# Gathering the next expert's rows earlier in an mLSTM-plus-routing kernel

## Chip, core and metric

One core of a Trainium2 chip. The metric is the device time in microseconds of one execution; for the kernel before it is 405.84 us, the median of three (404.99 to 406.05). One more execution was recorded by the hardware profiler; its span is 402.9 us, and all positions in time below are counted from the start of that span.

The core's engines run side by side, each with its own queue of instructions: TensorE (PE in the profile; its weight loads are PEld), VectorE (DVE), ScalarE (ACT), GpSimd (POOL), and SyncE (SP), which issues transfers. [...]

## What is computed

First an mLSTM cell over `(4, 8, 768, 40)`, whose output, as 3072 rows of 320 numbers, is then routed to one of eight experts by a hash of the token:

```python
def _moe_ref(x, token_ids, w1, w2) -> np.ndarray:
    N, D = x.shape                       # 3072, 320
    E = w1.shape[0]                      # 8; w1 is (8, 320, 1024), w2 is (8, 1024, 320)
    expert_idx = token_ids * np.int64(2654435761) % np.int64(E)
    out = np.zeros((N, D), dtype=np.float32)
    for e in range(E):
        mask = expert_idx == e
        if not mask.any():
            continue
        xe = x[mask]
        h = np.maximum(xe @ w1[e], 0.0)
        out[mask] = h @ w2[e]
    return out.astype(np.float32)
```

All of it is in float32. The change lies where the mLSTM ends and the experts begin.

## The kernel before

The mLSTM writes its rows to `x_rows` (`x_d`) in device memory. Each expert gathers the rows that belong to it (three tiles of 128 and 32 remainders, 416 in all), turns them so that the 320 features lie on the partitions, and runs two layers.

Expert 0 is special. Its rows are gathered before the last 256 rows have been stored; what it has of those comes as a product with a table of ones (`om`), and is added at the end. `spin0` runs products that nobody reads.

```python
        rows_by_table(0, 0)
        xo = back(LB, NB - 1)
        rows_by_table(0, 1)
        rows_by_table(0, 2)
        finish(LB, NB - 1, xo)()                  # stores the last rows to x_d
        for i, j in enumerate((NJ, *range(NJ))):
            ...
            for db in range(2):
                nc.tensor.transpose(tp[:, db, :n], xg0[:n, j, db * P : (db + 1) * P], ident[:n, :n])
            nc.scalar.copy(xg0[:n, j, Dm:], xg0[:n, j, 2 * P : Dm])
            nc.tensor.transpose(tp[:, 2, :n], xg0[:n, j, 2 * P :], ident[:n, :n])
            nc.scalar.copy(xT0[:, :, j * P : j * P + n], tp[:, :, :n])       # L904
            if i < DB:
                rows_by_table(1, i)
            if i == DB - 1:
                spin0(1)
        spin0(2)
        for db in range(DB):
            nc.vector.tensor_tensor(xT0[:, db, :], xT0[:, db, :], om[db][:, :CAP], op=ALU.add)   # L911
```

The turn of a tile for the later experts. For expert 1 a small copy on VectorE first doubles the last 64 columns (`copied` is false); from expert 2 on ScalarE has done that before.

```python
    def turn(xg, dst, on_act, copied=False):
        tp = mps.tile([P, DB, P], F32, name="tp", tag="bank")
        for db in range(2):
            nc.tensor.transpose(tp[:, db, :], xg[:, db * P : (db + 1) * P], ident[:])
        if not copied:
            nc.vector.tensor_copy(xg[:, Dm:], xg[:, 2 * P : Dm])             # L944
        nc.tensor.transpose(tp[:, 2, :], xg[:, 2 * P :], ident[:])
        ...                                                                  # copy to dst, ScalarE or VectorE
```

Layer 1 of expert 0 goes over four pairs of feature blocks. `between(fp)` is where a turn may be put in: inside the even pairs, and after the odd ones.

```python
            if fp % 2 == 0:
                for i in range(2):
                    whole(i, True)                # L968, four products
                between(fp)
                halves(False)                     # L961
                for i in range(2):
                    out(i)
            else:
                halves(True)
                for i in range(2):
                    whole(i, False)
                    out(i)
                between(fp)
```

Layer 2 calls `between(0)` after its first plain product, `between(1)` after the middle of a scheme of seven products with sums, and `between(2)` at its end:

```python
        scatter(zp, idx(2), True)
        between(0)
        ...
        product(yb, s2, t2, False)
        nc.vector.tensor_tensor(u2[:], yb, p1[:], op=ALU.add)                # L1148
        between(1)
        product(xb, s1, t1, False)
        nc.vector.tensor_tensor(u3[:], xa, u2[:], op=ALU.add)                # L1151
        nc.vector.tensor_tensor(z1[:, DH:], xb, u3[:], op=ALU.add)           # L1152
        product(ya, a[0][1], half(1, 0), False)
        nc.scalar.copy(z0[:, :DH], ya)
        product(xa, a[1][1], t4, False)
```

And the loop over the experts with what comes before it. `fetch(e)` gathers on GpSimd (L919); `sums_of_w2` is four GpSimd operations (L1105); `turns(1)` is a list of four turns: tiles 0, 1, 2 and the remainders; `sums_of_x` is five VectorE operations on the turned rows of the next expert.

```python
        sums = sums_of_w2(W[0][2])
        fetch(1)

        for piece in weight_slices(1):
            piece(nc.scalar)
        ...
        for e in range(E):
            ...
            ahead = turns(e + 1) if e + 1 < E else []

            def one(fp):
                if ahead and (e > 0 or fp != 0 or len(ahead) < 4):
                    ahead.pop(0)()

            def after(j):
                if j == (e == 0) and e + 1 < E:
                    xss[e + 1] = sums_of_x(xTs[e + 1])
                one(j)
                ...
            if e == 0:
                layer1(W[e], xTs[e], h, CAP, one)
            else:
                layer1_pairs(W[e], wsums, xTs[e], xss[e], h, one)
            ...
            layer2_pair(W[e], sums, h, cols_of(s_idx, e * NJ), after)
```

A scheduler may place an engine's instructions in another order than the program's, so the built kernel's order is read beside the code.

Of the kernel before, what the change touches and what calls it, by code (L numbers as in the profile page):

```python
# [22 lines left out]
def kernel(  # L23
# [30 lines left out]
    E, _, F = moe_w1.shape  # L54
# [9 lines left out]
    DB = len(dch)  # L64
# [52 lines left out]
    def weight_slices(e):  # L117

        W[e], slices = weights(moe_w1[e], moe_w2[e], wpools[e % 3 > 0], w2pools[e % 6 > 0])
        return slices  # L120
# [8 lines left out]
    with tc.tile_pool(name="gates", bufs=1) as gp, \  # L129
# [107 lines left out]
        def piece(z, j, r, src, eng):  # L237
            if eng is nc.scalar:
                nc.scalar.copy(z[r, j, :], src)
            else:  # L240
                nc.gpsimd.tensor_copy(z[r, j, :], src)
# [449 lines left out]
        one = gp.tile([P, 2, 1], F32, name="one")  # L691
# [188 lines left out]
        def rows_by_table(k, db):  # L880
            nc.tensor.matmul(
                om[db][:, :CAP], lhsT=xl[:, k, db * P : (db + 1) * P], rhs=ones0[:, k, :], start=(k == 0), stop=(k == 1),
                skip_group_check=True,
            )


        def spin0(n):
            idle = ps.tile([P, CAP], F32, name="idle", tag="tr", bufs=4)
            for _ in range(n):
                nc.tensor.matmul(idle[:], lhsT=ident[:], rhs=W[0][0][:, 0, :CAP], start=True, stop=True)  # L890
# [6 lines left out]
        for i, j in enumerate((NJ, *range(NJ))):  # L897
            n = RM if j == NJ else P
            tp = ps.tile([P, DB, P], F32, name="tp0", tag="tr", bufs=4)
# [4 lines that stand above are left out]
            nc.scalar.copy(xT0[:, :, j * P : j * P + n], tp[:, :, :n])  # L904
            if i < DB:
                rows_by_table(1, i)
            if i == DB - 1:
                spin0(1)
        spin0(2)
        for db in range(DB):  # L910
            nc.vector.tensor_tensor(xT0[:, db, :], xT0[:, db, :], om[db][:, :CAP], op=ALU.add)  # L911

# [5 lines left out]
    def gather(xg, idx):  # L918
        nc.gpsimd.indirect_dma_start(  # L919
            out=xg, out_offset=None, in_=x_d[:, :], in_offset=bass.IndirectOffsetOnAxis(ap=idx, axis=0),  # L920
        )

    def scatter(zp, idx, apart):
        zo = xp.tile([P, Dm], F32, name="zo", bufs=4)
        nc.scalar.copy(zo[:], zp[:])
        send(zo, idx, apart)
# [11 lines left out]
# [8 lines that stand above are left out]
        if on_act:  # L946
            nc.scalar.copy(dst, tp[:])
        else:
            nc.vector.tensor_copy(dst, tp[:])
        return tp  # L950
# [56 lines left out]
    def sums_of_w1(w1t):  # L1007

        a = [[w1t[:, k, :].rearrange("p (a i f) -> p i a f", i=2, f=P)[:, i] for k in range(2)] for i in range(2)]
        s1, s2, s3, s4 = s = [xp.tile([P, FB // 2, P], F32, name=f"ws{i}", bufs=1) for i in range(1, 5)]  # L1010
        ops = ((s1, a[1][0], a[1][1], ALU.add), (s2, s1[:], a[0][0], ALU.subtract),
               (s3, a[0][0], a[1][0], ALU.subtract), (s4, a[0][1], s2[:], ALU.subtract))
        return s, [lambda o=o: nc.gpsimd.tensor_tensor(o[0][:], o[1], o[2], op=o[3]) for o in ops]  # L1013
# [86 lines left out]
    def sums_of_w2(w2t):  # L1100

        b = [[w2t[:, k::2, c * DH : (c + 1) * DH] for c in range(2)] for k in range(2)]
        t1, t2, t3, t4 = (xp.tile([P, FB // 2, DH], F32, name=f"t{i}", bufs=1) for i in range(1, 5))
        for d, x, y in ((t1, b[0][1], b[0][0]), (t2, b[1][1], t1), (t3, b[1][1], b[0][1]), (t4, b[1][0], t2)):
            nc.gpsimd.tensor_tensor(d[:], x, y[:] if y in (t1, t2) else y, op=ALU.subtract)  # L1105
        return t1, t2, t3, t4
# [56 lines left out]
    def cols_of(t, c0):  # L1163
        return lambda j: t[:, c0 + j : c0 + j + 1]

    with tc.manual_schedule():
        xgs, xTs, remT, hrem = {}, {0: xT0}, {}, {}

        def fetch(e):
            if e % EG == 0 or e == 1:  # L1170
                xgs[-1 - e // EG] = xp.tile([P, DB * P], F32, name="xr")
            xgs[e] = xp.tile([P, NJ, DB * P], F32, name="xg", bufs=3)
            for j in range(NJ):
                gather(xgs[e][:, j, :Dm], cols_of(g_idx, e * NJ)(j))
            if e % EG == 0 or e == 1:
                gather(xgs[-1 - e // EG][:, :Dm], cols_of(g_idx, NR + e // EG)(0))

        def turns(e):
            xT = xTs[e] = xp.tile([P, DB, CAP], F32, name="xT")

            def tile_of(j):
                turn(xgs[e][:, j, :], xT[:, :, j * P : (j + 1) * P], j % 2 == 1, e > 1)

            def remainder():
                i = e % EG
                if i == 0 or e == 1:
                    remT[e // EG] = xp.tile([P, DB, P], F32, name="remT")
                    turn(xgs[-1 - e // EG], remT[e // EG][:], True, e > 1)
                nc.scalar.copy(xT[:, :, NM:], remT[e // EG][:, :, i * RM : (i + 1) * RM])

            return [lambda j=j: tile_of(j) for j in range(NJ)] + [remainder]

        def rest(g):
            zp = mps.tile([P, Dm], F32, name="zp", tag="bank")
            for fb in range(FB):
                for i in range(EG):
                    nc.tensor.matmul(
                        zp[i * RM : (i + 1) * RM, :], lhsT=hrem[g][:, i, fb, :], rhs=W[g * EG + i][2][:, fb, :],
                        start=(fb == 0), stop=(fb == FB - 1),
                    )  # L1200
            scatter(zp, cols_of(s_idx, NR + g)(0), True)

        sums = sums_of_w2(W[0][2])
        fetch(1)


        for piece in weight_slices(1):
            piece(nc.scalar)
        wsums, pieces, xss = None, [], {}
        for e in range(E):  # L1210
            g, i = e // EG, e % EG
            if e + 2 < E:
                fetch(e + 2)
            if e > 0:
                sums = sums_of_w2(W[e][2])
            h = xp.tile([P, FB, CAP], F32, name="h", bufs=1)
            if i == 0:
                hrem[g] = xp.tile([P, EG, FB, RM], F32, name="hrem")
            ahead = turns(e + 1) if e + 1 < E else []

            def one(fp):
                if ahead and (e > 0 or fp != 0 or len(ahead) < 4):
                    ahead.pop(0)()

            def after(j):
                if j == (e == 0) and e + 1 < E:
                    xss[e + 1] = sums_of_x(xTs[e + 1])
                one(j)
                if j == 0 and i == EG - 1:
                    rest(g)  # L1230

            if e + 1 < E:
                wnext, pieces = sums_of_w1(W[e + 1][0])
# [4 lines that stand above are left out]
            for piece in pieces:  # L1238
                piece()
            pieces = []  # L1240
            nc.scalar.copy(hrem[g][:, i], h[:, :, NM:])
            layer2_pair(W[e], sums, h, cols_of(s_idx, e * NJ), after)
            wsums = wnext

            if e + 2 < E:
                for j in range(NJ):
                    nc.scalar.copy(xgs[e + 2][:, j, Dm:], xgs[e + 2][:, j, 2 * P : Dm])
                if (e + 2) % EG == 0:
                    xr = xgs[-1 - (e + 2) // EG]
                    nc.scalar.copy(xr[:, Dm:], xr[:, 2 * P : Dm])  # L1250
            if e + 3 < E:
                slices = weight_slices(e + 3)
                if e == 0:
                    slices[1:1] = weight_slices(2)
                for piece in slices:
                    piece()
# [51 lines left out]
```

## Time and profile before

| engine | busy, us | share of the 402.9 us |
|---|---|---|
| TensorE, products | 378.4 | 94% |
| TensorE, weight loads | 311.6 | 77% |
| VectorE | 221.3 | 55% |
| GpSimd | 201.3 | 50% |
| ScalarE | 148.8 | 37% |

The mean clock granted to TensorE was 0.983 of full speed. TensorE's products in layer 1 of expert 0 begin at 167.82 us; the last scatter of output rows starts at 395.92 us.

A line of the timeline gives start, duration (both in us), engine, line, operation, target and sources, shape, and how many instructions are merged; in brackets stand the idle time of the engine just before, and what ended it. A line of waits gives who waited for whom: total us, times, the longest. A line of the table by windows gives a stretch and its length, then the busy time and number of instructions of PE, PEld, DVE, ACT and POOL, the granted clock, the share of the DMA engines and GB/s.

### The profile page before, as it was taken

To read this page: it belongs to the slowest core of one execution; us is meant where nothing else is said; L and a number is where in the kernel's file an instruction comes from. 1 tells how busy PE (TensorE), PEld (TensorE's weight loads), DVE (VectorE), ACT (ScalarE), POOL (GpSimd) and SP (SyncE) were. 2 spreads that over 40 slices of the span, in tenths; PEclk is the share of its full clock that TensorE was granted. 3 is DMA by queue.
4 is the path that set the end of the run, shared out by engine and by line. 5 is a ranking of instruction groups with operands and counts; after the bars stand their busy time and mean duration, and the time that the engine had idled before them with its cause. 6 is when DMAs were issued, how large, how long until landed. Compare 5 with 4: busy or idle time off the path is not lost. (4 is left out here: it accounts for less than half of the span.)

```text
span 402.9 us, 8802 instructions
## 1 busy us (share of the span) xinstructions
PE 378.4 (94%) x3397; PEld 311.6 (77%) x3397; DVE 221.3 (55%) x537; ACT 148.8 (37%) x290; POOL 201.3 (50%) x253
## 2 busy tenths in 40 slices
PE   8789979999999997899999999999999999999991
PEld 8668868877877774457898978978979989889780
DVE  8657557778797984133447356462455463453500
ACT  6335785575676541222132231141131141321310
POOL 6653103324535634881295593871692874807011
PEclk9969999999999999999999999999999999999996
DMA  7588846977767513835938245244244200000000
GB/s 150 111 174 190 205 107 152 242 197 176 151 149 182 132 65 126 285 83 164 333 129 272 75 130 171 83 130 152 83 142 142 78 16 33 2 15 34 0 17 36
DMA packets 96616, 51.53 MB, mean 128 GB/s; under 512 B 68455, under 2 KB 90604, under 8 KB 96572
## 3 DMA queue, kind: packets, MB, share of 16 engines
q1 hardware_dynamic: 90956, 39.29, 37.8%
q0 software_dynamic: 2528, 8.24, 6.2%
q10 hardware_dynamic: 3088, 3.41, 2.8%
q8 instruction: 28, 0.46, 0.5%
q14 instruction: 16, 0.13, 0.1%
HBM read 42.02 MB, written 8.65 MB: 126 GB/s over the span
## 5 line engine op out<-in xcount | busy, mean ns | idle before, releaser
L929 POOL DMA_INDIRECT out_dram<-zo,s_idx x26 | 26.9, 1035 | 91.5 <-DVE zo L1159 53.2
L476 POOL TENSOR_TENSOR x<-x,den 128x320 f32<-128x320 f32 x21 | 15.1, 723 | 48.8 <-DVE den L474 27.4
L387 DVE TENSOR_TENSOR w<-sp,w 128x512 f32<-128x512 f32 x48 | 30.9, 686 | 12.6 <-PE sp L379 12.0
L1121 PE MATMUL zp<-w2t,h 128*128 128x320 f32 x128 | 36.5, 438 | 0.0
L379 PE MATMUL sp<-qT,kT 64*128 64x128 f32 x384 | 29.4, 291 | 2.7 <-ACT qT L316 1.5
L379 PEld LDWEIGHTS sp<-qT,kT 64*128 64x128 f32 x384 | 24.6, 193 | 9.3 <-issue 4.6
L1121 PEld LDWEIGHTS zp<-w2t,h 128*128 128x128 f32 x128 | 23.2, 190 | 11.1 <-issue 1.8
L1091 ACT ACTIVATE h<-h 128x832 f32<-128x832 f32 x14 | 12.6, 898 | 47.6 <-DVE h L1090 47.6
L342 ACT ACTIVATE w<-ab 128x512 f32<-128x512 f32 x48 | 26.6, 608 | 7.5 <-PE ab L338 7.5
L1131 PE MATMUL zp<-t,s 128*128 128x160 f32 x192 | 27.5, 299 | 0.6 <-DVE s L1116 0.6
L437 PE MATMUL ht<-w,v 128*64 128x128 f32 x384 | 27.1, 285 | 0.0
L1131 PEld LDWEIGHTS zp<-t,s 128*128 128x128 f32 x192 | 26.5, 190 | 0.8 <-POOL ws L1013 0.8
L1105 POOL TENSOR_TENSOR t<-w2t 128x640 f32<-128x640 f32 x16 | 24.8, 1548 | 1.7 <-PE tp L901 1.6
L1105 POOL TENSOR_TENSOR t<-w2t,t 128x640 f32<-128x640 f32 x16 | 24.7, 1545 | 0.6
L1039 PE MATMUL mb<-xs,ws 128*128 128x208 f32 x112 | 25.0, 346 | 0.0
L1039 PE MATMUL ma<-xT,w1t 128*128 128x208 f32 x112 | 24.8, 346 | 0.0
L437 PEld LDWEIGHTS ht<-w,v 128*64 128x64 f32 x384 | 21.2, 140 | 4.0 <-issue 3.3
L919 POOL DMA_INDIRECT xg<-x_rows,g_idx x21 | 20.3, 966 | 6.2 <-issue 5.8
L449 ACT COPY hB<-ht 128x512 f32<-128x512 f32 x20 | 11.7, 587 | 30.8 <-PE ht L437 29.2
L1039 PEld LDWEIGHTS mb<-xs,ws 128*128 128x128 f32 x112 | 19.6, 190 | 1.8 <-issue 1.8
L458 PE MATMUL xo<-ident,hB 128*128 128x128 f32 x96 | 16.3, 298 | 4.3 <-ACT hB L449 2.2
L1039 PEld LDWEIGHTS ma<-xT,w1t 128*128 128x128 f32 x112 | 18.9, 190 | 1.8 <-issue 1.8
(261 smaller groups left out, 888.7 us busy)
## 6 DMA issues: line engine op xcount, KB each, us to landing
w2t<-in_moe_w_dram SPq DMA_DIRECT2D x28, 320.0 KB
w1t<-in_moe_w_dram SPq DMA_DIRECT2D x28, 256.0 KB
k<-in_k_dram SPq DMA_DIRECT2D x24, 160.0 KB
v<-in_v_dram SPq DMA_DIRECT2D x24, 160.0 KB
x_rows<-x SPq DMA_DIRECT2D x22, 160.0 KB
ql<-in_q_dram SPq DMA_DIRECT2D x6, 480.0 KB
og<-in_o_gate_dram SPq DMA_DIRECT2D x6, 480.0 KB
w1c<-in_moe_w_dram SPq DMA_DIRECT2D x14, 128.0 KB
```

What stands on the lines that cost most here:

```text
L342: nc.scalar.activation(w[:, hf], ab[:], AF.Exp)
L379: nc.tensor.matmul(sp[hf][:, j, :], lhsT=d["kT"][r, j, :], rhs=q_of(s)[r, j, :], start=True, stop=True,)
L387: nc.vector.tensor_tensor(d["w"][:, hf], d["sp"][hf][:], d["w"][:, hf], op=ALU.mult)
L437: nc.tensor.matmul(place(j, hf), lhsT=d["v"][:, 2 * j + hf, :], rhs=d["w"][:, hf, j, :], start=(c == 0 and j0 == 0), stop=True, skip_group ...
L458: nc.tensor.transpose(xo[:, hf, i, :], src[:, hf, i, :], ident[:])
L476: eng.tensor_tensor(xv, xv, den[:].to_broadcast([P, 2, PR, D]), op=ALU.mult)
L919: nc.gpsimd.indirect_dma_start(out=xg, out_offset=None, in_=x_d[:, :], in_offset=bass.IndirectOffsetOnAxis(ap=idx, axis=0),)
L929: ins = nc.gpsimd.indirect_dma_start(out=out[:, :], out_offset=bass.IndirectOffsetOnAxis(ap=idx, axis=0), in_=zo[:], in_offset=None, bound ...
L1039: nc.tensor.matmul(dst[:, i, :], lhsT=x(2 * q + i), rhs=y, start=(start and i == 0), stop=stop, skip_group_check=True,)
L1105: nc.gpsimd.tensor_tensor(d[:], x, y[:] if y in (t1, t2) else y, op=ALU.subtract)
L1121: nc.tensor.matmul(zp[:], lhsT=h[:, fb, 2 * P : 3 * P], rhs=w2t[:, fb, :], start=(fb == 0), stop=(fb == FB - 1),)
L1131: nc.tensor.matmul(dst, lhsT=x[:, i], rhs=y[:, i], start=(start and i == 0), stop=(i == FB // 2 - 1), skip_group_check=True,)
```

## The change

Three things around expert 0. Of the three unread products one is left, after the last turn, to keep TensorE occupied while the copy and the additions run. The gathers of expert 1 are issued ahead of the sums of `w2`, so that its rows come sooner. And the turns of expert 1 start at the first pair of layer 1, one at each pair, so that all four are done when layer 2 begins; `sums_of_x` then can stand at `between(0)` for expert 0 as it does for the others.

```diff
             if i < DB:
                 rows_by_table(1, i)
-            if i == DB - 1:
-                spin0(1)
-        spin0(2)
+        spin0(1)
         for db in range(DB):
             nc.vector.tensor_tensor(xT0[:, db, :], xT0[:, db, :], om[db][:, :CAP], op=ALU.add)
 ...
+        fetch(1)
         sums = sums_of_w2(W[0][2])
-        fetch(1)
 ...
-            def one(fp):
-                if ahead and (e > 0 or fp != 0 or len(ahead) < 4):
+            def one(_):
+                if ahead:
                     ahead.pop(0)()

             def after(j):
-                if j == (e == 0) and e + 1 < E:
+                if j == 0 and e + 1 < E:
                     xss[e + 1] = sums_of_x(xTs[e + 1])
                 one(j)
```

Two lines go from the part before the experts, so the line numbers after it are lower by two in the changed kernel (L944 is L942 there, L911 is L909).

## The prediction

> **What bounds the kernel now.** I read four views in this order: the page's first two parts, the waits of TensorE, the order in time of the stretch around the first expert, and the DMA queues there. The first says that TensorE carries the time, so only what moves TensorE's instructions counts.
>
> ```profile
> PE 378.4 (94%) x3397; PEld 311.6 (77%) x3397; DVE 221.3 (55%) x537; ACT 148.8 (37%) x290; POOL 201.3 (50%) x253
> ...
> PE   8789979999999997899999999999999999999991
> ...
> PEclk9969999999999999999999999999999999999996
> ```
>
> TensorE is full from slice 17 on. The clock row has one dip, in the third slice, which matters below. The waits of TensorE from 167 us to the end are three, 2.3 us in all; everything else there is back to back:
>
> ```profile
> PE mh L968 <- DVE both L911: 0.9, 1, 0.9
> PE zp L1131 <- DVE zo L1152: 0.8, 1, 0.8
> PE zp L1131 <- DVE s L1116: 0.6, 1, 0.6
> ```
>
> The stretch that the change touches, from the timeline (start, duration, instruction, idle time before it):
>
> ```profile
> 164.35 0.86 PE L890 MATMUL idle<-w1t,ident 128*128 128x416 f32 x2
> 165.05 0.38 PE L901 MATMUL tp<-ident,both 128*128 128x128 f32 x2
> 165.27 0.27 PE L903 MATMUL tp<-ident,both 128*128 128x128 f32 x1
> 165.38 1.56 PE L890 MATMUL idle<-w1t,ident 128*128 128x416 f32 x4
> ...
> 165.58 0.48 ACT L904 COPY both<-tp 128x384 f32<-128x384 f32 x1 [1.10 <-PE tp L903]
> ...
> 166.09 1.08 DVE L911 TENSOR_TENSOR both<-both,sp 128x416 f32<-128x416 f32 x2 [5.26 <-ACT both L904]
> 167.09 0.58 DVE L911 TENSOR_TENSOR both<-both,ht 128x416 f32<-128x416 f32 x1
> 167.31 0.96 POOL L919 DMA_INDIRECT xg<-x_rows,g_idx  x1
> ...
> 167.82 3.03 PE L968 MATMUL mh<-both,w1t 128*128 128x416 f32 x8 [0.88 <-DVE both L911]
> ```
>
> The chain to the first expert is: last transpose, copy out (L904), three additions (L911, 166.09 to 167.67), then layer 1 at 167.82. One unread product takes 0.70 us (164.35 to 165.05). GpSimd does the four sums of w2 first and only then gathers the next expert's rows, from 167.31.
>
> [...] TensorE was busy 1.67 us of 17.0 to 20.5, and the clock was 0.51 and 0.50 in the next two stretches of the table by windows, 1.00 after them. The drop lasted about 6.8 us[...]:
>
> ```profile
> 17.00:20.50 3.50, 1.67 (x23) 1.23 (x22) 3.40 (x8) 1.71 (x4) 2.50 (x5) 1.00 0.98 181
> 20.50:24.00 3.50, 2.33 (x21) 1.71 (x19) 3.43 (x8) 0.86 (x2) 2.56 (x9) 0.51 0.30 63
> 24.00:27.40 3.40, 3.40 (x30) 2.85 (x26) 1.33 (x3) 0.69 (x3) 0.75 (x4) 0.50 1.05 269
> ```
>
> [...] VectorE's instructions stand in time as they stand in the built kernel. [...] from 160.75 to 162.75 the weights of the next expert and the gather share the engines (47.6% and 27.4%).
>
> **The change, part by part.**
>
> *Two unread products less.* They go from L890; one stays, behind the last transposes. The first of the three stood before those transposes, so they could come 0.70 us earlier, and with them L904, the additions and layer 1. The other removed one filled time in which TensorE waits anyway. Worth −0.7 us, if the additions wait for nothing else.
>
> *Gathers ahead of the sums.* Four gathers of the next expert (three tiles and the remainders) come before the four sums. They cannot start when the sums started (161.01): they read rows whose last store is issued at 160.87. The waits of SyncE's queue name that store's landing, 4.1 us after, so at 165.0. So they start at 165.05 instead of 167.31, 2.3 us sooner. The sums (6.15 us) then run from about 170 to 176; layer 2 reads them at 189.4, so that costs nothing.
>
> *Turns from the first pair on.* Four turns at the four pairs instead of three, with the remainders' turn after the first product of layer 2. The number of transposes is the same; 0.33 us each on TensorE, moved, not removed. The sums of x move from between(1) to between(0) of layer 2. At between(1) the five of them stood on VectorE from 192.06 to 193.91, ahead of the L1151 and L1152 for which TensorE waited 0.77 us. At between(0) they fall into VectorE's idle 4.78 us before L1148. Worth −0.77 us.
>
> So the plan taken alone is −0.70 − 0.77 = −1.5 us. But the order of the built kernel shows something that the diff doesn't. On VectorE the changed kernel has, by its own line numbers,
>
> ```
> L942 TensorCopy xg<-xg 128x64      waits for the first gather
> L909 TensorTensor both<-both,sp 128x416
> L909 TensorTensor both<-both,sp 128x416
> L909 TensorTensor both<-both,ht 128x416
> L947 TensorCopy xT<-tp 128x3x128
> ```
>
> The small copy of tile 0's last 64 columns (L944 before, L942 now), which the turn of tile 0 needs, has been placed **ahead of the three additions**. Before, it stood behind two evictions of layer 1, at 174.59, when the rows had long landed. [...] the additions, and with them layer 1 of expert 0, now wait for the first gather of expert 1.
>
> When does that land? In the DMA queues by quarter microseconds, the first gather before (issued 167.31, weights just ending) moved its 160 KB until 170.3, 2.9 us after issue. The last gather of expert 0 (issued 158.47, with weights beside it) until 162.5, 4.0 us. The receipt adds some 0.45 us: the last store's bytes ended at 164.55 and its landing was seen at 165.0. The queue of weights is at 96.1% from 165.0 to 169.5, so the gather will share. Landing is 165.05 + 3.4 to 4.5 = 168.4 to 169.5; I take 169.05.
>
> - Small copy 0.18 us: to 169.25.
> - Three additions as before, 167.67 − 166.09 = 1.58 us: to 170.85.
> - 0.15 us to the first product, as before (167.67 to 167.82): layer 1 starts at 171.0, against 167.82. **+3.2 us.** The 0.70 us are lost in this wait.
> - TensorE's last work before that is the one unread product, ending at about 165.6. It then idles 5.4 us. [...] the trace dropped the clock at 48% busy. So the first part of layer 1 runs at half rate. The earlier drop lasted 6.8 us; here part of it may fall into the idle time. I take 4 us of half rate, in which half the work is lost: **+2.0 us** (0.9 to 3.4).
> - The vanished wait in layer 2: **−0.8 us**.
>
> Sum +4.4 us; 405.84 + 4.4 = **410.2 us**. Nothing behind it gives it back: after 167 us TensorE has almost no idle time to shorten.
>
> **The rivals.**
>
> 1. *The plan works.* The copy's place does no harm because the gather lands by 165.5. Then 404.4 us. For it speaks only the intent; against it, the gather cannot even be issued before the store lands at 165.0.
> 2. *The late start without the cold clock.* 405.84 + 3.2 − 0.8 = 408.2 us. For it: an idle time of 1.53 us at 158.6 left the clock at 1.00. Against: this one is over three times as long.
> 3. *A long stall.* Weights crowd the gather out, it lands at 170 or after, [...]: 4.2 + 3.4 − 0.8 = +6.8, 412.6 us. For it: the 96.1%. Against: in the trace a gather beside the weights still finished in 4.0 us.
> 4. *GpSimd becomes the bound.* Its sums and gathers of expert 0 end at about 185 instead of 181. The first scatter of layer 2 comes after 188 in any case, so I give this nothing.
>
> **Range and chances.** The low end joins the fast landing (168.4), the small clock loss (0.9) and the full −0.8: 405.84 + 2.55 + 0.9 − 0.8 = 408.5; a little below for rival 2: 408.0. The high end is rival 3: 412.5. The 2% limits lie at 397.7 and 414.0. No rival reaches the first; the second needs more than rival 3. So: faster 0.01, within 2% 0.95, slower 0.04.
>
> **What would show it.** In the changed profile VectorE's L942 should start at about 169 after a long wait for a gather, and L909 directly behind it. The first L966 should come at about 171, with TensorE idle over 5 us and some 4 us at a clock of 0.5 after it. The gathers (L917) should start at about 165, and the 0.77 us wait in layer 2 should be gone. If L909 starts at about 165.4, the reading of the order was wrong and rival 1 holds. If the clock stays at 1.00 across the gap, rival 2 holds.

## The result and the profile after

The changed kernel takes 411.0 us (median of four, 409.8 to 411.61) beside 405.94 for the kernel before; the ratio is 1.0121, 95% interval 1.0084 to 1.0157. It is slower by about 5 us. Timed again on another chip it was 411.02 us, ratio 1.0130 (1.0094 to 1.0166).

The page of the changed kernel, parts 1 and 2 (busy time and share, then the span in 40 slices):

```profile
PE 379.2 (93%) x3393; PEld 311.7 (76%) x3393; DVE 224.6 (55%) x537; ACT 148.7 (36%) x290; POOL 200.9 (49%) x253
...
PE   8759979999999999299999999999999999999991
...
PEclk9988999999999999889999999999999999999998
```

TensorE's busy time hardly changed, but slice 17 of its row is now a 2 where it was an 8, and the clock row has a second dip just there. The waits of TensorE from 160 us on (who waited for whom: us in total, times, longest) name the cause:

```profile
PE mh L966 <- DVE both L909: 6.0, 1, 6.0
PE tp L901 <- DMA both<-x_rows,g_first: 1.3, 2, 0.9
PE zp L1129 <- DVE s L1114: 0.6, 1, 0.6
...
```

The wait of layer 1 for the additions grew from 0.9 to 6.0 us, and the 0.8 us wait in layer 2 (L1152 before, L1150 now) is gone. The timeline of the same profile shows what the additions waited for:

```profile
166.17 0.94 POOL L917 DMA_INDIRECT xg<-x_rows,g_idx  x1 [4.00 <-PE ht L881]
...
167.24 0.86 PE L890 MATMUL idle<-w1t,ident 128*128 128x416 f32 x2
...
167.44 0.48 ACT L904 COPY both<-tp 128x384 f32<-128x384 f32 x1 [0.42 <-PE tp L903]
...
170.25 2.24 DVE L942 COPY xg<-xg 128x64 f32<-128x64 f32 x1 [8.89 <-DMA xg<-x_rows,g_idx]
170.89 1.54 POOL L1103 TENSOR_TENSOR t<-w2t 128x640 f32<-128x640 f32 x1
172.41 1.07 DVE L909 TENSOR_TENSOR both<-both,sp 128x416 f32<-128x416 f32 x2
...
173.41 0.57 DVE L909 TENSOR_TENSOR both<-both,ht 128x416 f32<-128x416 f32 x1
```

```profile
174.13 4.57 PE L966 MATMUL mh<-both,w1t 128*128 128x416 f32 x8 [6.03 <-DVE both L909]
```

The last line is from TensorE's own timeline: layer 1 starts after 6.03 us without work. The operands of the additions were ready when L904 ended at 167.92. VectorE stood at L942 until the gather landed at 170.25, and then for 2.24 us at the copy itself. By windows (stretch, length, busy PE, PEld, DVE, ACT, POOL, then the clock, the DMA share and GB/s), the clock falls to half; the shares 0.60 and 0.69 put the fall at 170.4 and the return at 177.2:

```profile
168.00:170.00 2.00, 0.10 (x1) 0.00 (x0) 0.00 (x0) 0.00 (x0) 1.39 (x3) 1.00 0.77 222
170.00:172.00 2.00, 0.00 (x0) 0.00 (x0) 1.75 (x1) 0.00 (x0) 1.97 (x2) 0.60 1.05 378
172.00:174.00 2.00, 0.00 (x0) 0.00 (x0) 1.99 (x4) 0.00 (x0) 1.92 (x2) 0.50 0.91 348
174.00:176.00 2.00, 1.87 (x3) 1.18 (x4) 0.00 (x0) 0.00 (x0) 2.00 (x3) 0.50 0.05 18
176.00:178.00 2.00, 2.00 (x5) 0.98 (x4) 0.00 (x0) 0.00 (x0) 1.85 (x2) 0.69 0.00 0
```

A caution about whole times. The mLSTM part has its own dips of the clock, and they differ from execution to execution: from 20 to 30 us the mean clock was 0.66 in the first profile of before and 0.83 in that of changed, from 30 to 40 us 1.00 and 0.83. The last turn of the mLSTM before the final one (L458, four transposes) starts anywhere from 153.9 to 156.7 us in the profiles. So I also compare each profile in two stages. Stage A runs from that L458 to the first product of layer 1 of expert 0, stage B from there to the end of the span.

| kernel | stage A, us | first 8 records of layer 1, us | stage B, us | ratio of times (95% interval) |
|---|---|---|---|---|
| before, first profile | 13.94 | 3.03 | 235.1 | |
| before_again | 12.99 | 3.03 | 236.3 | |
| changed | 17.85 | 4.57 | 235.7 | 1.0121 (1.0084 to 1.0157) |
| after_again | 18.34 | 5.40 | 236.6 | 1.0130 (1.0094 to 1.0166) |
| copy_behind_additions | 13.11 | 3.03 | 234.6 | 0.9991 (0.9974 to 1.0008) |
| copy_on_scalar | 13.56 | 3.03 | 235.7 | 1.0025 (1.0007 to 1.0044) |
| turns_from_second_pair | 13.20 | 3.03 | 235.0 | 1.0007 (0.9987 to 1.0026) |
| turns_from_second_late_gathers | 12.96 | 3.03 | 234.9 | 1.0008 (0.9987 to 1.0030) |
| sums_after_all_gathers | 17.00 | 4.81 | 235.9 | 1.0109 (1.0069 to 1.0150) |
| eight_unread | 18.16 | 4.72 | 235.8 | 1.0076 (1.0049 to 1.0103) |
| ten_unread | 18.66 | 3.03 | 234.1 | 1.0093 (1.0058 to 1.0128) |
| one_unread_only | 12.87 | 3.03 | 235.1 | 0.9988 (0.9967 to 1.0009) |
| sums_in_gap | 13.46 | 3.03 | 235.1 | 0.9980 (0.9965 to 0.9995) |
| sums_in_gap_copies_on_gpsimd | 13.68 | 3.03 | 234.7 | 0.9988 (0.9972 to 1.0003) |

The loss is in stage A, 17.85 and 18.34 us against 12.99 and 13.94, and at the start of stage B, where the first 8 records of layer 1 take 4.57 and 5.40 us instead of 3.03.

### The profile page after: what moved, and what is told of

Same layout as the page of the kernel before. It is cut to its first block, busy times and chain, and to the rows that moved or that the text cites. A ratio compares the mean times of both kernels' runs of the same rounds, so it can differ in the third digit from the quotient of the medians.

```text
span 409.8 us, 8796 instructions
## 1 busy us (share of the span) xinstructions
PE 379.2 (93%) x3393; PEld 311.7 (76%) x3393; DVE 224.6 (55%) x537; ACT 148.7 (36%) x290; POOL 200.9 (49%) x253
## 5 line engine op out<-in xcount | busy, mean ns | idle before, releaser
L476 POOL TENSOR_TENSOR x<-x,den 128x320 f32<-128x320 f32 x21 | 15.1, 724 | 48.7 <-DVE den L474 27.4
L449 ACT COPY hB<-ht 128x512 f32<-128x512 f32 x20 | 11.7, 587 | 29.8 <-PE ht L437 27.3
L1129 PE MATMUL zp<-w2t,h 128*128 128x160 f32 x128 | 20.2, 301 | 0.0
```

The source lines that it names most:

```text
L476: eng.tensor_tensor(xv, xv, den[:].to_broadcast([P, 2, PR, D]), op=ALU.mult)
L1129: nc.tensor.matmul(dst, lhsT=x[:, i], rhs=y[:, i], start=(start and i == 0), stop=(i == FB // 2 - 1), skip_group_check=True,)
```

## The experiments

### Is it the place of the copy?

Two kernels keep everything of the change and only take tile 0's copy out of VectorE's way.

```diff
 copy_behind_additions: tied to the third addition's result, tile 0 only
-            nc.vector.tensor_copy(xg[:, Dm:], xg[:, 2 * P : Dm])
+            nc.vector.scalar_tensor_tensor(
+                xg[:, Dm:], in0=xT0[:, 2, :DP], scalar=0.0, in1=xg[:, 2 * P : Dm], op0=ALU.mult, op1=ALU.add)
 copy_on_scalar: all four copies of expert 1
-            nc.vector.tensor_copy(xg[:, Dm:], xg[:, 2 * P : Dm])
+            nc.scalar.copy(xg[:, Dm:], xg[:, 2 * P : Dm])
```

> The changed kernel, with tile 0's small copy tied behind the third addition on VectorE (it also multiplies a piece of that result by 0 and adds it, so that no scheduler can place it ahead). Order theory: the additions run as soon as the last rows are turned, TensorE does not idle for more than about 2 us before layer 1, the clock stays at 1.00 there, and the time falls by all of the loss and to the plan's gain: about 404.4 us, ratio to the kernel before about 0.996. Rival, the early gathers themselves (they crowd expert 0's gather or stall the first turn): the time stays above 408, with TensorE waiting for a transfer at the last turns or at tile 0's transposes.

> The changed kernel, with expert 1's small copies on ScalarE. Order theory: as with the copy behind the additions, about 404.4 us; no copy stands on VectorE at all, and the additions follow the last turn directly. Rival, the early gathers themselves: above 408. If ScalarE's queue is what it harms instead (the copy waits there ahead of layer 1's evictions), TensorE would stall at the second half of the first pairs, about 406.

Measured: 405.54 us, ratio 0.9991, and 406.35 us, ratio 1.0025. VectorE and TensorE in copy_behind_additions, from the two engines' timelines:

```profile
168.05 1.08 DVE L909 TENSOR_TENSOR both<-both,sp 128x416 f32<-128x416 f32 x2 [6.31 <-ACT both L904]
169.06 0.58 DVE L909 TENSOR_TENSOR both<-both,ht 128x416 f32<-128x416 f32 x1
170.44 0.23 DVE L942 SCALAR_TENSOR_TENSOR xg<-both,xg 128x64 f32<-128x64 f32 x1 [0.81 <-DVE both L909]
```
```profile
169.78 3.03 PE L970 MATMUL mh<-both,w1t 128*128 128x416 f32 x8 [1.58 <-DVE both L909]
172.65 0.38 PE L940 MATMUL tp<-ident,xg 128*128 128x128 f32 x2
```

The additions now wait for L904 alone, layer 1 starts 0.14 us behind them, and the turn of tile 0 at 172.65 waits for nothing. With the same early gathers and the same turn at the first pair, the whole loss is gone. That settles the cause, against the rival of the early gathers. But neither kernel reached the expected 404.4 us: the plan's gain is missing, which the later runs explain. (In copy_behind_additions the 0.8 us wait in layer 2 is gone, but 0.3 us of waiting for the remainders' copy is new.) On ScalarE the copies add two waits of TensorE for them (0.5 us for tile 1, 0.5 us for the remainders).

A third way is to leave the first pair without a turn, as in the kernel before; a fourth also puts the gathers back behind the sums.

```diff
 turns_from_second_pair
-            def one(_):
-                if ahead:
+            def one(fp):
+                if ahead and (e > 0 or fp != 0):
+                    ahead.pop(0)()
+                if e == 0 and fp == 3 and ahead:
                     ahead.pop(0)()
 turns_from_second_late_gathers: that, and
-        fetch(1)
         sums = sums_of_w2(W[0][2])
+        fetch(1)
```

> The changed kernel with its early gathers, but no turn at the first pair and two at the fourth, so that tile 0's copy stands behind the first evictions again, as in the kernel before. Order theory: the loss is gone without any change to the copy; the 0.8 us wait in layer 2 stays away: 405.0 to 405.5 us. Rival, the early gathers cost time themselves: 407 or more.

> As turns_from_second_pair, but with the gathers of expert 1 behind the sums of w2, as in the kernel before. If the early gathers bring nothing as long as no turn needs them sooner: the same as turns_from_second_pair within the interval, about 405 us. If they cost time by crowding the last gather of expert 0 or the weights: up to 0.5 us less than it.

Measured: 405.27 us, ratio 1.0007, and 405.3 us, ratio 1.0008. The loss is gone in both, and the place of the gathers makes no difference that these intervals show. Both keep a new 0.5 us wait of TensorE for the remainders' copy at the fourth pair, which eats most of what the 0.8 us wait in layer 2 gave.

### Why did the copy take 2.24 us?

```diff
 sums_after_all_gathers: expert 2's gathers also ahead of the sums
         fetch(1)
+        fetch(2)
         sums = sums_of_w2(W[0][2])
 ...
-            if e + 2 < E:
+            if e > 0 and e + 2 < E:
                 fetch(e + 2)
```

> The changed kernel with expert 2's three gathers also ahead of the sums of w2, so that GpSimd runs no tensor operation when tile 0's small copy runs on VectorE. Theory that the copy's 2.24 us come from a GpSimd tensor operation that it has to wait out: the copy takes about 0.2 us, layer 1 starts some 2 us sooner, about 409.0 us. Rival, the copy's length comes from the transfer (rows still landing) or from itself: 2.2 us as before and 411.0 us.

> The changed kernel, unchanged, timed on the chip of the next two and profiled a second time. All theories: 410 to 411 us. In the profile tile 0's small copy waits for its gather again; if the theory holds that it also waits out a GpSimd tensor operation, its end falls within 0.1 us of the end of one, and is not 2.24 us long as such.

Measured: 409.94 us, ratio 1.0109, and 411.02 us, ratio 1.0130. VectorE and GpSimd in sums_after_all_gathers, and then in after_again:

```profile
169.54 0.94 POOL L917 DMA_INDIRECT xr<-x_rows,g_idx  x1 [0.30 <-issue]
170.47 0.20 DVE L942 COPY xg<-xg 128x64 f32<-128x64 f32 x1 [10.06 <-DMA xg<-x_rows,g_idx]
170.58 1.08 DVE L909 TENSOR_TENSOR both<-both,sp 128x416 f32<-128x416 f32 x2
170.79 0.95 POOL L917 DMA_INDIRECT xg<-x_rows,g_idx  x1 [0.30 <-issue]
```
```profile
169.45 1.54 POOL L1103 TENSOR_TENSOR t<-w2t 128x640 f32<-128x640 f32 x1
169.94 1.11 DVE L942 COPY xg<-xg 128x64 f32<-128x64 f32 x1 [10.52 <-DMA xg<-x_rows,g_idx]
170.97 1.07 DVE L909 TENSOR_TENSOR both<-both,sp 128x416 f32<-128x416 f32 x2
171.06 1.54 POOL L1103 TENSOR_TENSOR t<-w2t,t 128x640 f32<-128x640 f32 x1
```

With only gathers on GpSimd the copy takes 0.20 us. With a tensor operation there, it ends when that ends: 169.94 + 1.11 = 171.05 against 169.45 + 1.54 = 170.99; in the changed kernel's first profile 172.49 against 172.43. The copy is not slow as such; it ends with the operation beside it. By what means is not shown, and the order of the recorded starts does not decide it: the copy starts ahead of the tensor operation in the changed kernel's first profile (170.25 against 170.89) and behind it in after_again (169.94 against 169.45), and both times it ends 0.06 us after it.

The expected 409.0 us was not reached. Stage A of sums_after_all_gathers is only 0.9 us shorter than in the changed kernel's first profile and 1.3 us shorter than in its second: against the first, its gather was issued 0.6 us later, counted from that L458, and took 0.6 us longer to land.

### What does the clock cost?

```diff
-        spin0(1)
+        spin0(8)      # eight_unread; spin0(10) in ten_unread
```

> The changed kernel with eight unread products instead of one, 4.9 us more of work that falls into TensorE's 6.0 us of idle time. Clock theory: the start of layer 1 stays where it is, the clock stays at 1.00 and the first products of layer 1 take 0.35 us each instead of 0.70: about 1.6 us less than the changed kernel, 409.4 us. Rival, the clock costs nothing: 411.0, and if the unread products run past the additions, later.

> The changed kernel with ten unread products, so that TensorE has no idle time over about 1 us before layer 1. With eight it still had 2.2 us, and the clock still fell for 3.4 us. Clock theory: now the clock stays at 1.00, the first eight records of layer 1 take 3.0 us instead of 4.7, and the time is 1.6 us below eight unread products: 406.8. Rival, the fall of the clock comes from the kind of work or the whole stretch before: as with eight, 408.4, or above where the products run past the additions.

Measured: 408.37 us, ratio 1.0076, and 409.88 us, ratio 1.0093. Eight unread products leave TensorE 2.2 us idle, and the clock falls to 0.50 all the same; ten leave 0.85 us, and it stays at 1.00 in every stretch from 165 to 180 us. The first products of layer 1, in eight_unread and in ten_unread:

```profile
172.47 4.72 PE L966 MATMUL mh<-both,w1t 128*128 128x416 f32 x8 [2.18 <-DVE both L909]
```
```profile
172.67 3.03 PE L966 MATMUL mh<-both,w1t 128*128 128x416 f32 x8 [0.85 <-DVE both L909]
```

By windows, eight_unread again:

```profile
170.00:172.00 2.00, 0.29 (x1) 0.00 (x0) 2.00 (x4) 0.00 (x0) 1.92 (x2) 1.00 0.76 296
172.00:174.00 2.00, 1.53 (x3) 0.97 (x4) 0.32 (x1) 0.00 (x0) 2.00 (x3) 0.70 0.04 11
174.00:176.00 2.00, 2.00 (x4) 0.94 (x3) 0.00 (x0) 0.00 (x0) 1.85 (x2) 0.50 0.00 0
176.00:178.00 2.00, 2.00 (x10) 1.05 (x11) 0.44 (x1) 0.00 (x0) 1.43 (x2) 0.94 0.30 82
```

So in these profiles taking the idle time away (0.85 us left of 6.0) takes the fall of the clock away, and the fall costs 4.57 − 3.03 = 1.5 us in the changed kernel's first profile and 5.40 − 3.03 = 2.4 us in its second. Stage B confirms the size: less that term it is 234.1 us in changed, and 234.2 in after_again, as it is in ten_unread without any.

Why 1.5 and 2.4? The low clock lasted 6.8 us in both (from 170.4, and from 170.6), but layer 1 began at 174.13 and at 172.69, so only 3.1 and 4.8 us of it met work, of which, at a clock of 0.50, half is lost. The moment of the fall does not follow from the length of the pause alone: it came 2.3 and 4.6 us after TensorE's last work, and in eight_unread at 172.8, when the work had begun again (172.47); there it lasted 3.4 us.

The whole times show less. The kernel ten_unread was expected at 406.8 us and is not below eight_unread, but the intervals of the two ratios overlap, so their order is not shown. In the profile of ten_unread the gather landed 5.3 us after issue and stage A is 0.5 us longer than with eight. And the mean granted clock of whole executions was 0.974 in the ten runs of the changed kernel, 0.983 in the fourteen of eight_unread (0.979 in the profiled one), and 0.986 in the seven of ten_unread. In most runs of eight_unread the clock then probably did not fall at this place, and its time already holds that gain; this is inferred, not shown.

### Where did the plan's gain go?

```diff
 one_unread_only: the kernel before with
-            if i == DB - 1:
-                spin0(1)
-        spin0(2)
+        spin0(1)
 sums_in_gap: the kernel before with
             def after(j):
-                if j == (e == 0) and e + 1 < E:
+                if e == 0:
+                    one(j)
+                if j == 0 and e + 1 < E:
                     xss[e + 1] = sums_of_x(xTs[e + 1])
-                one(j)
+                if e > 0:
+                    one(j)
```

> The kernel before, unchanged, for a second profile of it. In the first one ScalarE's copy L449 sat idle for 1.64 us just ahead of expert 0's turns, which in none of the other profiles it does. Theory that the removed unread products hide behind expert 0's own gather: without that idle time TensorE waits for the last gathered tile at the last turns (0.3 to 1.0 us), as it does in the profiles of the changed kernel and its variants. Rival, they stood on the path: no such wait, and the last transposes start right after the first unread product.

> The kernel before with only the first part of the change: one unread product, behind the turns, instead of three. If the removed product stood on the path, as the prediction has it: 0.7 us less, 405.0. If expert 0's last gathered tile decides: no difference, 405.7, and TensorE waits 0.4 to 1.0 us for that tile at the last transposes instead.

> The kernel before with one thing moved: sums_of_x of expert 1 at between(0), directly behind the remainders' turn, instead of at between(1). No early gathers, no turn at the first pair, three unread products as before. If the 0.77 us wait in layer 2 is on the path: that wait disappears, nothing takes its place, and the time is 0.8 us below the kernel before, about 404.8. Rival, a new wait (TensorE for the sums, or for VectorE's u2): no difference.

Measured: one_unread_only 404.96 us, ratio 0.9988 (0.9967 to 1.0009); sums_in_gap 404.61 us, ratio 0.9980 (0.9965 to 0.9995). At the last turn of expert 0's rows, TensorE and then ScalarE in before_again, and TensorE in one_unread_only:

```profile
164.13 0.86 PE L890 MATMUL idle<-w1t,ident 128*128 128x416 f32 x2
164.83 0.38 PE L901 MATMUL tp<-ident,both 128*128 128x128 f32 x2
```
```profile
164.66 0.24 ACT L902 COPY both<-both 128x64 f32<-128x64 f32 x1 [0.55 <-DMA both<-x_rows,g_first]
```
```profile
164.79 0.41 PE L901 MATMUL tp<-ident,both 128*128 128x128 f32 x2 [0.46 <-DMA both<-x_rows,g_first]
```

In before_again ScalarE's L902 already waits for the last gathered tile; it starts at 164.66, just ahead of the transposes at 164.83. TensorE shows no wait only because the unread product fills the time. Without the product it waits 0.46 us for the transfer and starts at the same place: stage A is 12.87 us against 12.99. The removed product was not on the path. In the first profile of before this was hidden, because ScalarE's L449 idled 1.64 us just ahead, so that everything behind came late and the tile was there.

The moved sums are different. In sums_in_gap the 0.77 us wait is gone, and nothing took its place at that spot. Its waits from 152 us on:

```profile
PE mh L968 <- DVE both L911: 0.9, 1, 0.9
PE tp L945 <- DVE xg L944: 0.8, 1, 0.8
PE xo L458 <- ACT hB L449: 0.7, 1, 0.7
PE zp L1131 <- DVE s L1116: 0.6, 1, 0.6
PE tp L901 <- DMA both<-x_rows,g_first: 0.5, 2, 0.4
PE tp L903 <- ACT both L902: 0.3, 1, 0.3
```

It is the one version whose interval lies wholly below 1, and the only part of the change whose gain is shown. The second line is the long copy again: tile 0's copy took 1.81 us here and 1.95 us in before_again (where TensorE waited 0.9 us), and ended 0.05 and 0.07 us behind a GpSimd tensor operation (L1013). The last kernel tried to remove that too.

```diff
 sums_in_gap_copies_on_gpsimd: sums_in_gap with, for expert 1's three tiles,
-            nc.vector.tensor_copy(xg[:, Dm:], xg[:, 2 * P : Dm])
+            nc.gpsimd.tensor_copy(xg[:, Dm:], xg[:, 2 * P : Dm])
```

> As sums_in_gap, with the small copies of expert 1's three tiles on GpSimd, in its own queue between the last gather and the sums of w1, so that no copy of VectorE has to wait for a GpSimd tensor operation. In sums_in_gap and before_again VectorE's copy of tile 0 took 1.8 to 2.0 us and TensorE waited 0.8 to 0.9 us for it. Theory that this wait comes from the two engines meeting: it is gone, and the time is up to 0.8 us below sums_in_gap, 403.8 to 404.6. Rival, GpSimd's own copy comes too late (its last gather ends at about 174.8, TensorE needs the copy at 175.3): TensorE waits for GpSimd instead, no gain.

Measured: 405.82 us, ratio 0.9988 (0.9972 to 1.0003). The rival holds in part: TensorE waits 0.4 us for GpSimd's copy, which starts at 176.10, behind the last gather (175.14, 0.95 us), instead of 0.8:

```profile
PE tp L945 <- POOL xg L944: 0.4, 1, 0.4
```

No gain over sums_in_gap can be shown.

## Why the prediction was right

- *The copy's place makes the additions wait for the first gather.* Right, and shown by copy_behind_additions: the loss goes with it. In the five profiles with the copy in front the first addition starts 0.07 to 0.09 us ahead of the copy's recorded end (172.41 against 172.49 in the changed kernel's first).
- *Landing 3.4 to 4.5 us after issue.* The first profile had 4.1 us. The other four profiles with the copy in front had 4.7 to 5.3, so the estimate was rather low. The gather started at 166.17 us against 165.05. That it waits for the last store fits: SyncE's wait of 3.6 us for that store began at 161.7, when its issue was over, and ended at 165.3; the gather starts 0.9 us after that end. The prediction had allowed 0.05 us for this. Its 165.0 for the kernel before counted the wait from the start of the issue; from the end of it, at 161.18, it runs to 165.26, so what lies between the last bytes (164.55) and the landing is 0.7 us there, not 0.45.
- *Small copy 0.18 us.* Wrong: 2.24 and 1.11 us, both times with its end 0.06 us behind that of a GpSimd tensor operation. The step took a duration from the quiet case, though the profile of the kernel before has another L944 of 0.87 us (at 176.28). Landing and copy together were predicted as 4.2 us and measured as 6.32 in both profiles of the changed kernel. These 2.1 us are the largest mis-sized term behind the growth of stage A, which was predicted as 3.2 us and measured as 17.85 − 12.99 = 4.9 us against before_again (3.9 against the first profile of before). The late start of the gather added to it, and an earlier store took some back: it landed 9.0 us after that L458, against 11.4 in the profile that the prediction read.
- *Additions 1.58 us, then 0.15 us to layer 1.* Right: 172.41 to 173.98, layer 1 at 174.13.
- *Clock, +2.0 us (0.9 to 3.4).* Right, 1.5 and 2.4 us in size; as the prediction supposed, part of the low clock fell into the idle time. That the pause would bring a fall was the author's estimate from one earlier fall (0.51 and 0.50 from 20.5 to 27.4 us), and the 3.4 us of its high end and of rival 3 are half of the 6.8 us that it lasted. The changed kernel's two profiles show the fall, in pauses of 6.0 and 6.7 us.
- *The vanished wait, −0.8 us.* Right; the wait is gone, and sums_in_gap shows a gain in the time, −0.2% (−0.05 to −0.35).
- *Two unread products less, −0.7 us, if the additions wait for nothing else.* Wrong as part of rival 1, and harmless in the sum, where it was already counted as lost: expert 0's own gather decides there. Rival 1's 404.4 us was therefore too low; the repaired order gives 405.5.
- *Sum.* Predicted +4.4 us, measured +5.1. From the first profile: +4.9 in stage A against before_again, +1.5 clock, −0.8 wait makes 5.6. That the sum comes so close is partly luck: the terms that were too small (landing and copy) and too large (clock) partly cancel.

## What to carry to other kernels

Read the built order of each engine, not only the diff: an instruction moved earlier in the program can be placed ahead of work that it then blocks until a transfer lands (here layer 1 waited 6.03 us for the additions), and a tie to the result that must come first repairs it (1.58 us in copy_behind_additions). A filler product is worth removing only if the work behind it is ready sooner; look at what the other engines wait for at that point, since the filler can hide the wait (none on TensorE there in before_again, 0.46 us in one_unread_only). Take the duration of a small copy from the neighbourhood it will run in (2.24 and 1.11 us here), not from its quiet case (0.18 us).

## What the runs showed beside

- A 128x64 copy of VectorE took 0.18 to 0.23 us where the trace has no GpSimd tensor operation beside it, and 0.34 to 2.24 us in the twelve cases, recorded singly, where one ran. There its recorded end lies 0.05 to 0.07 us behind the end of that operation, even of one that started after the copy's recorded start (170.89 against 170.25). The additions took 0.5 to 0.6 us each beside a GpSimd tensor operation (changed, 172.41 to 173.98) and beside gathers (copy_behind_additions, 168.05 to 169.64).
- The clock fell after an idle time of 2.2 us (eight_unread) and did not after one of 1.6 us (copy_behind_additions). Where between them the limit lies, or whether there is one, no run shows.
- A gather of 160 KB landed 4.1 to 5.3 us after issue beside the stream of weights (five profiles with the copy in front).
